# Attention followed by two feed-forward blocks: decode of the first weights begun at unit 11, a step at every second unit until unit 38

## The chip, the cores and the metric

The kernel runs on one core of a Trainium2 chip. The metric is the time of one execution on the device, in microseconds (us). The engines are named as the profile names them: PE is TensorE's matmul and PEld its weight load, DVE is VectorE, ACT is ScalarE, POOL is GpSimd, and SP is SyncE, which here only issues DMAs.

## The reference

Twelve heads of causal attention over two sequences of 448 positions are followed by two blocks of layer norm and a feed-forward network, the second with a Fourier transform in front of it. The two weights of the second block come as float64.

```python
attn = softmax(mask(q @ k.T / sqrt(64))) @ v      # 2 x 12 heads, 448 positions, 64 wide
x = heads side by side                            # 2 x 448 x 768
xn = layer_norm(x) * g
x = x + relu(xn @ w1) @ w2                        # 768 -> 3072 -> 768
u = x + real(fft(fft(x, axis=1), axis=2))
un = layer_norm(u)
out = u + relu(un @ w3) @ w4
```

## The kernel before

All products are kept near float32 accuracy by splitting each operand into a high and a low part and multiplying three times (lines 93 to 95, `mm3`).

**Weights.** They arrive as float64 bits in 96 tiles of 128 x 768 and are turned into two float32r halves by `w_tile`, a generator of four steps: step 1 is an ACT scaling copy (L164) and a DVE shift (L165), step 2 a DVE instruction (L167), step 3 another (L171), step 4 an ACT copy (L89, the high half) and a DVE subtraction (L90, the low half). `w_load` issues the DMA of one raw tile (`wraw`, L147) on the SP queue, 768 KB each. `w_step` runs one step and then loads ahead; `w_tick(n, upto)` runs up to n steps while fewer than `upto` tiles are begun. Raw tiles and the query, key and value tiles of a head pair (`qkv`, `load_pair`) share six slots of one pool, `praw`; the working bits (`wbits`) have two, the finished halves (`wsp`) six.

**Attention.** There are 12 pairs of heads and four units in each pair, so 48 units; the loop runs over `i`, one unit each. A unit's scores (`sps`, L279) get their row minimum on DVE (L296, with `maskw`, in the fourth unit with `maskf`), the exponentials on ACT (`pexp`, L308), transposes on PE (`tps`, L345), a copy on ACT (`pT`, L350), and the product with the values on PE (`avps`, L364). Once a pair, DVE forms the reciprocal row sums (L316, L317), POOL spreads them on a diagonal (`diag`, L322), PE turns these into rows (`invps`, L334), ACT copies them (`inv`, L339), and DVE scales the values (L389) and adds to the sum for the layer norm (`lnacc`, L414). Splitting the queries is work for POOL (L238, L239, L242), splitting the keys for ACT and DVE (`ks`, L250, L251). There is one bank for `avps`: the next pair's values wait for L389.

In the last third of the loop the layer norm of the first sequence runs beside it (`lnm` L428, `xc` L436, `xn` L456 and L466). Here too, in the kernel before, the loads of the first weights begin (from unit 32) and their decode (a step per unit from unit 38). After the loop the first matmuls of the feed-forward block (`hps`, L93 to L95) use the first five tiles, and in their midst stands the layer norm's sum for the second sequence (`lnm`), which needs the last L414.

**Order.** A scheduler places the instructions of each engine while the kernel is built: it follows the program's order as a priority but moves an instruction whose inputs it expects earlier into a place that it expects empty. So a decode step of unit 38 can stand beside unit 31. On the chip each engine runs its list in order and waits at its head.

Of the kernel before, what the change touches and what calls it, by code (L numbers as in the profile page):

```python
# [28 lines left out]
UNITS = [((0, 0, 0, 0, 0), (0, 2, 0, 128, 128)), ((1, 0, 0, 0, 0), (1, 2, 0, 128, 128)),  # L29
         ((0, 1, 0, 0, 0), (1, 1, 1, 0, 256)), ((None, 3, 0, 0, 0),)]  # L30
ES = 4
W_LOAD, W_FROM, W_EARLY = 32, 38, 6
SPLIT_AT = {1: (1, 1), 2: (2, 5)}
AHEAD, L_T, L_C, L_V = (3, 1, 2, 3)
Q_AT, K_AT = (0, 1)
# [17 lines left out]
def fused_kernel(ctx: ExitStack, tc: tile.TileContext, aps, out):  # L53
# [86 lines left out]
    n_raw, n_split = [0], [0]  # L140
# [47 lines left out]
    def w_tick(n=3, upto=None):  # L188
        for _ in range(n):
            if w_now or n_split[0] < min(w_low[0] + WSLOTS, upto or len(order)):  # L190
                w_step()
# [26 lines left out]
    def load_pair(b, pr):  # L218
        t = praw.tile([P, 2 * NM * P], F32, tag="r", name="qkv")
        q_raw[b, pr] = t[:, : 2 * S].rearrange("p (a s) -> p a s", a=2)  # L220
        v_raw[b, pr] = t[:, 2 * S : 2 * S + 8 * D].rearrange("p (r k d) -> p r k d", r=2, k=4)
        if (b, pr) == pairs[0]:
            nc.scalar.dma_start(out=q_raw[b, pr][:, 1], in_=aps["qk"][b, pr][:, 1])
            nc.sync.dma_start(out=q_raw[b, pr][:, 0], in_=aps["qk"][b, pr][:, 0])
        else:
            nc.sync.dma_start(out=q_raw[b, pr], in_=aps["qk"][b, pr])
        nc.sync.dma_start(out=v_raw[b, pr], in_=aps["v2"][b, pr])
# [60 lines left out]
    def row_max(i):  # L288

        b, pr, unit = units[i]  # L290
        if i % len(UNITS) == 0:
            stat[b, pr] = psm.tile([P, 3, NT], F32, tag="st", name="stat")
        for col, at, c, _, n in widths(unit):
            o = s_ps[i][at][:, c : c + n]
            mask = maskf if unit[0][0] is None else maskw
            last = nc.vector.tensor_tensor_reduce(  # L296
                out=o, in0=o, in1=mask[:, mask.shape[1] - n :], scale=1.0, scalar=1e38, op0=ALU.add, op1=ALU.min,
                accum_out=stat[b, pr][:, 0, col : col + 1],
            )
        return last  # L300

    def exps(i):
        b, pr, unit = units[i]
        e = exp_tiles[i % ES]
        flat = e.rearrange("p a b -> p (a b)")
        sp, st = s_ps.pop(i), stat[b, pr]
        for col, at, c, to, n in widths(unit):
            nc.scalar.activation(  # L308
                out=flat[:, to : to + n], in_=sp[at][:, c : c + n], func=ACTF.Exp, scale=-1.0, bias=st[:, 0, col : col + 1],
                accum_out=st[:, 1, col : col + 1],  # L310
            )
        p_sb[i] = e
# [28 lines left out]
    def transposes(i):  # L341
        e = p_sb.pop(i)
        tp = bank("tps")
        for a in range(4):
            nc.tensor.transpose(out=tp[:, a * P : (a + 1) * P], in_=e[:, a], identity=ident)  # L345
        t_ps[i] = tp

    def transposed(i):
        t = t_tile([P, 4, P], "pT", F32)
        nc.scalar.activation(  # L350
            out=t.rearrange("p a q -> p (a q)"), in_=t_ps.pop(i), func=ACTF.Copy
        )
        pT[i] = t
# [336 lines left out]
    i = 0  # L690
    while i < n + L_V or max(later, default=0) >= i:
        pi, at = divmod(i, per)
        if 0 <= i - L_T < n:
            transposes(i - L_T)
        while scored <= min(i + AHEAD, n - 1) and units[scored][:2] in kparts:
            scores(scored)
            scored += 1
        if i < n:
            red = row_max(i)
        if 0 <= i - L_C < n:  # L700
            transposed(i - L_C)
        for f in later.pop(i, []):
            f()
        if i == 0:
            exps(0)
        for f, p in splits.pop(i, []):
            for _ in f(*pairs[p]) or ():
                pass
        if at == 2 and pi + 3 < len(pairs):
            load_pair(*pairs[pi + 3])  # L710
        if i >= W_LOAD and n_raw[0] < n_split[0] + 2:
            w_load()
        if i >= W_FROM:
            w_tick(1, W_EARLY)
        with tc.issue_after(red.ins):
            bg_step()
        if 0 < i < n:
            exps(i)
        if 0 <= i - L_V < n:
            values(i - L_V)  # L720
            b, pr, _ = units[i - L_V]
            if (i - L_V) % per == per - 1:
                scaled(b, pr)
                ln_sum(b, pr, xa)
                if pr >= HJ:
                    later.setdefault(i + 1, []).append(lambda b=b, pr=pr: moved(b, pr))
                if (b, pr) == (0, PAIRS[-1]):
                    later.setdefault(i + 1, []).append(lambda: ln_first())
        if i < n and i % per == per - 1:
            b, pr, _ = units[i]  # L730
            later.setdefault(i + 1, []).append(lambda b=b, pr=pr: (sum_recip(b, pr), spread(b, pr)))
            later.setdefault(i + 3, []).append(lambda b=b, pr=pr: spread_rows(b, pr))
        i += 1
# [138 lines left out]
```

## Time and profile before

| What | us |
|---|---|
| median of three runs (860.02 to 862.39) | 860.39 |
| the profiled execution | 860.33 |
| its span, first to last instruction | 858.6 |
| start of the fourth unit's row minimum, pair 3 (of 0 to 11) | 24.62 |
| last L317 of the attention | 106.07 |
| first matmul of the feed-forward block | 110.02 |
| DVE busy over the span | 602.6 (70%) |
| PE busy over the span | 842.1 (98%) |

PE's busy share is modelled from pipelined matmuls and is no sign of work at its peak. To read the start of the kernel, cut it at the fourth unit's row minimum of each pair (L296 with `maskf`, which is the same instruction in each pair): these lie at 24.62, 32.53, 40.55, 48.58, 56.20, 65.20, 74.41, 82.51, 93.65 and 102.17 us, and a pair's stretch is what lies between two of them. I count them as stretch 3 (24.62 to 32.53) to stretch 11 (93.65 to 102.17). What comes after 110 us is one block of matmuls after another, to the end of the span.

### The profile page before, as it was taken

The numbers are of one execution on the slowest core, as the hardware profiler recorded it, in microseconds if no ns is written. First come the engines' busy times: TensorE is split into PE (matmuls) and PEld (weight loads), VectorE is DVE, ScalarE is ACT, GpSimd is POOL, SyncE is SP. The second block draws the span as 40 slices with busy tenths as digits, with TensorE's granted clock in tenths as the row PEclk, the third lists the DMA queues.
The fourth block names the chain that finished last, engine by engine and source line by source line (L and its number), as shares of the span: only waits on it lengthen the run. The fifth ranks groups of instructions, "written<-read, shape, count | busy, mean of one in ns | idle before, by whom it ended". The sixth has DMA issues, their size and how long they took to land.

```text
span 858.6 us, 11890 instructions
## 1 busy us (share of the span) xinstructions
PE 842.1 (98%) x4688; PEld 754.7 (88%) x4688; DVE 602.6 (70%) x995; ACT 329.3 (38%) x615; POOL 70.5 (8%) x102
## 2 busy tenths in 40 slices
PE   6999899999999999999999999999999999999997
PEld 5766689999999999999998889899999999999997
DVE  5779999796666666656699789697666566666433
ACT  6889874323332233223333245322332233223200
POOL 5665300100000000000100000100000000000000
PEclk9999899999999999999999999999999999999999
DMA  5433444424333333332625202324333333320011
GB/s 202 136 105 130 164 180 148 146 74 148 111 111 111 110 111 107 110 101 95 216 73 197 74 1 87 134 69 151 100 104 108 104 104 110 111 74 0 1 65 65
DMA packets 21399, 93.25 MB, mean 109 GB/s; under 512 B 2750, under 2 KB 4550, under 8 KB 21344
## 3 DMA queue, kind: packets, MB, share of 16 engines
q1 hardware_dynamic: 19152, 86.68, 29.5%
q0 software_dynamic: 2048, 5.59, 2.1%
q8 instruction: 37, 0.61, 0.3%
q10 hardware_dynamic: 144, 0.23, 0.1%
q14 instruction: 18, 0.15, 0.1%
HBM read 88.36 MB, written 2.75 MB: 106 GB/s over the span
## 4 chain that ended last, share of the span: by engine, by line
PE 90%; DVE 4%; ACT 4%; issue 1%; DMA 0%; ACTq 0%; DVEq 0%
PE yps L93 14%; PE yps L95 14%; PE yps L94 14%; PE hps L95 14%; PE hps L93 14%; PE hps L94 14%; ACT pexp L308 2%; PE sps L279 1%; PE avps L364 1%; PE tps L345 1%; DVE sps L296 1%; ACT pT L350 1%; PE mixps L93 1%; PE mixps L94 1%; PE mixps L95 1%
## 5 line engine op out<-in xcount | busy, mean ns | idle before, releaser
L93 PE MATMUL yps<-h,wsp 128*128 128x448 f32 x576 | 211.2, 367 | 0.0
L93 PE MATMUL hps<-xn,wsp 128*128 128x448 f32 x576 | 211.0, 366 | 0.0
L95 PE MATMUL hps<-xn,wsp 128*128 128x448 f32 x576 | 210.9, 366 | 0.0
L94 PE MATMUL yps<-h,wsp 128*128 128x448 f32 x576 | 210.7, 366 | 0.0
L94 PE MATMUL hps<-xn,wsp 128*128 128x448 f32 x576 | 210.5, 366 | 0.0
L95 PE MATMUL yps<-h,wsp 128*128 128x448 f32 x576 | 210.4, 365 | 0.0
L89 ACT ACTIVATE wsp<-wbits 128x768 fp32r<-128x768 f32 x96 | 80.8, 842 | 174.4 <-PE yps L95 159.2
L164 ACT ACTIVATE wbits<-wraw 128x768 f32<-128x768 f32 x96 | 86.3, 899 | 96.5 <-DVE wsp L90 96.5
L93 PEld LDWEIGHTS hps<-xn,wsp 128*128 128x128 f32 x576 | 108.2, 188 | 9.3 <-issue 0.4
L94 PEld LDWEIGHTS yps<-h,wsp 128*128 128x128 f32 x576 | 108.2, 188 | 9.1 <-issue 0.6
L95 PEld LDWEIGHTS hps<-xn,wsp 128*128 128x128 f32 x576 | 108.2, 188 | 9.1 <-issue 0.2
L94 PEld LDWEIGHTS hps<-xn,wsp 128*128 128x128 f32 x576 | 108.2, 188 | 9.0 <-issue 0.2
L93 PEld LDWEIGHTS yps<-h,wsp 128*128 128x128 f32 x576 | 108.2, 188 | 8.9 <-issue 0.4
L95 PEld LDWEIGHTS yps<-h,wsp 128*128 128x128 f32 x576 | 108.2, 188 | 8.8 <-issue 0.2
L507 ACT ACTIVATE h<-hps 128x448 fp32r<-128x448 f32 x96 | 52.0, 543 | 149.7 <-PE hps L95 149.6
L508 DVE SCALAR_TENSOR_TENSOR h<-hps,h 128x448 fp32r<-128x448 f32 x96 | 59.3, 620 | 69.6 <-ACT h L507 69.5
L90 DVE TENSOR_TENSOR wsp<-wbits,wsp 128x768 fp32r<-128x768 f32 x96 | 94.2, 981 | 19.0 <-ACT wsp L89 14.1
L529 DVE TENSOR_TENSOR x<-x,yps 128x448 f32<-128x448 f32 x96 | 58.8, 616 | 68.3 <-PE yps L95 68.3
L165 DVE TENSOR_SCALAR wbits<-wbits 128x768 uint32<-128x768 uint32 x96 | 53.5, 557 | 63.4 <-ACT wbits L164 62.7
L167 DVE SCALAR_TENSOR_TENSOR wbits<-wraw,wbits 128x768 uint32<-128x768 uint32 x96 | 91.7, 955 | 2.3
L171 DVE SCALAR_TENSOR_TENSOR wbits<-wraw,wbits 128x768 uint32<-128x768 uint32 x96 | 92.0, 959 | 0.5
L308 ACT ACTIVATE pexp<-sps,stat 128x128 f32<-128x128 f32 (+3 forms) x84 | 42.0, 516 | 11.6 <-DVE stat L296 11.0
(116 smaller groups left out, 665.1 us busy)
## 6 DMA issues: line engine op xcount, KB each, us to landing
wraw<-in_w SPq DMA_DIRECT2D x96, 768.0 KB, 4.2
qkv<-in_qk SPq DMA_DIRECT2D x11, 448.0 KB, 5.4
qkv<-in_v SPq DMA_DIRECT2D x12, 256.0 KB, 5.8
out_t<-x SPq DMA_DIRECT2D x12, 224.0 KB, 1.9
x<-xr POOLq DMA_DIRECT2D x6, 222.2 KB, 3.4
cd<-in_cd POOLq DMA_DIRECT2D x3, 386.0 KB, 4.1
sd<-in_sd POOLq DMA_DIRECT2D x3, 386.0 KB, 5.9
cs<-in_cs POOLq DMA_DIRECT2D x2, 448.0 KB, 5.8
```

The costliest lines, as they stand in the source:

```text
L89: nc.scalar.activation(out=hi, in_=src, func=ACTF.Copy)
L90: nc.vector.tensor_tensor(out=lo, in0=src, in1=f32(hi), op=ALU.subtract)
L93: nc.tensor.matmul(out=dst, lhsT=w_lo, rhs=x_hi, start=first, stop=False)
L94: nc.tensor.matmul(out=dst, lhsT=w_hi, rhs=x_lo, start=False, stop=False)
L95: nc.tensor.matmul(out=dst, lhsT=w_hi, rhs=x_hi, start=False, stop=last)
L164: nc.scalar.activation(out=f, in_=high.bitcast(F32), func=ACTF.Copy, scale=EXPONENTS)
L165: nc.vector.tensor_scalar(out=bits, in0=bits, scalar1=3, scalar2=None, op0=ALU.logical_shift_left)
L167: nc.vector.scalar_tensor_tensor(out=bits, in0=high, scalar=0x80000000, in1=bits, op0=ALU.bitwise_and, op1=ALU.bitwise_or)
L171: nc.vector.scalar_tensor_tensor(out=bits, in0=low, scalar=29, in1=bits, op0=ALU.logical_shift_right, op1=ALU.bitwise_or)
L308: nc.scalar.activation(out=flat[:, to : to + n], in_=sp[at][:, c : c + n], func=ACTF.Exp, scale=-1.0, bias=st[:, 0, col : col + 1], accum_ ...
L508: nc.vector.scalar_tensor_tensor(out=t[:, 1], in0=src, scalar=0.0, in1=f32(t[:, 0]), op0=ALU.max, op1=ALU.subtract)
L529: nc.vector.tensor_tensor(out=xx, in0=xx, in1=y, op=ALU.add)
```

## The change

A constant is added and two conditions are widened:

```diff
-W_LOAD, W_FROM, W_EARLY = 32, 38, 6
+W_LOAD, W_TWO, W_FROM, W_EARLY = 10, 32, 38, 6
...
-        if i >= W_LOAD and n_raw[0] < n_split[0] + 2:
+        if i >= W_LOAD and n_raw[0] < n_split[0] + (2 if i >= W_TWO else 1):
             w_load()
-        if i >= W_FROM:
+        if i >= W_FROM or i > W_LOAD and i % 2:
             w_tick(1, W_EARLY)
```

The first raw tile is now asked for at unit 10, and at units 11, 13, ... 37 one step of the decode is run; from unit 38 there is one per unit as before. Still at most six tiles are begun in the loop. Fourteen steps are added ahead of unit 38, which is three and a half tiles; with these, all six are decoded inside the loop. Nothing is computed that was not computed before.

The scheduler's lists change with it. The first place is on DVE in stretch 3, behind the fourth unit's row minimum (`stat` rows are the second half of a row minimum). Before:

```order
L251 SCALAR_TENSOR_TENSOR ks<-qkv,ks 128x448
L316 TENSOR_SCALAR stat<-stat 128x7
L317 RECIPROCAL stat<-stat 128x7
L296 ISA sps,stat<-sps,maskw 128x128
L296 ISA stat 128x1
```

and now:

```order
L251 SCALAR_TENSOR_TENSOR ks<-qkv,ks 128x448
L165 TENSOR_SCALAR wbits<-wbits 128x768
L167 SCALAR_TENSOR_TENSOR wbits<-wraw,wbits 128x768
L296 ISA sps,stat<-sps,maskw 128x128
L296 ISA stat 128x1
L316 TENSOR_SCALAR stat<-stat 128x7
```

Two decode instructions of the first tile stand ahead of the row minima of the next pair now, and a third, L171, behind the stretch's L389.

The second place is the end of the attention on DVE, from the last fourth unit's row minimum on. Before:

```order
L296 ISA sps,stat<-sps,maskf 128x448
L296 ISA stat 128x1
L90 TENSOR_TENSOR wsp<-wbits,wsp 128x768
L165 TENSOR_SCALAR wbits<-wbits 128x768
L167 SCALAR_TENSOR_TENSOR wbits<-wraw,wbits 128x768
L316 TENSOR_SCALAR stat<-stat 128x7
L171 SCALAR_TENSOR_TENSOR wbits<-wraw,wbits 128x768
L317 RECIPROCAL stat<-stat 128x7
L165 TENSOR_SCALAR wbits<-wbits 128x768
L389 TENSOR_TENSOR x<-avps,inv 128x448
L90 TENSOR_TENSOR wsp<-wbits,wsp 128x768
L414 TENSOR_TENSOR lnacc<-lnacc,x 128x448
```

and now:

```order
L296 ISA sps,stat<-sps,maskf 128x448
L296 ISA stat 128x1
L171 SCALAR_TENSOR_TENSOR wbits<-wraw,wbits 128x768
L165 TENSOR_SCALAR wbits<-wbits 128x768
L167 SCALAR_TENSOR_TENSOR wbits<-wraw,wbits 128x768
L389 TENSOR_TENSOR x<-avps,inv 128x448
L316 TENSOR_SCALAR stat<-stat 128x7
L171 SCALAR_TENSOR_TENSOR wbits<-wraw,wbits 128x768
L414 TENSOR_TENSOR lnacc<-lnacc,x 128x448
L317 RECIPROCAL stat<-stat 128x7
L389 TENSOR_TENSOR x<-avps,inv 128x448
L414 TENSOR_TENSOR lnacc<-lnacc,x 128x448
```

L389 and the L414 of the pair before the last stand ahead of the last L317 now, not behind it, and no decode stands any more between the last L317 and the last L414.

The third place is the SP queue from the load of pair 5 on. `DMAHW6` and `DMAHW7` are the lanes of the DMAs; in the list of now the first raw tile takes lane 6 and the second lane 7. Before:

```order
L226 DMA qkv<-in_qk 128x896 [waits DMAHW4_49]
L227 DMA qkv<-in_v 128x512 [waits DMAHW5_49]
L226 DMA qkv<-in_qk 128x896 [waits DMAHW6_49,DVE_49,PE_49]
L227 DMA qkv<-in_v 128x512 [waits DMAHW7_49]
L226 DMA qkv<-in_qk 128x896 [waits DMAHW0_49,DVE_49,PE_49]
```

and now:

```order
L226 DMA qkv<-in_qk 128x896 [waits DMAHW4_49]
L227 DMA qkv<-in_v 128x512 [waits DMAHW5_49]
L147 DMA wraw<-in_w_0 128x1536 [waits DMAHW6_49,DVE_49,PE_49]
L147 DMA wraw<-in_w_0 128x1536 [waits DMAHW7_49,DVE_49,PE_49]
L226 DMA qkv<-in_qk 128x896 [waits DMAHW0_49,DMAHW6_49,DVE_49,Activation_49]
```

The load of pair 6 (the third row of before, the last of now) had a slot that an earlier pair gave up; it takes that of the first raw tile now, and so waits until ACT and DVE have decoded that tile.

## Rows read from the trace of the kernel before

**Rows 1.** Stretch, length, busy us (xcount) of PE, PEld, DVE, ACT, POOL, clock, DMA.

```profile
24.62:65.20 40.58, 39.73 (x441) 28.92 (x437) 30.31 (x99) 34.54 (x109) 26.66 (x35) 1.00 0.37 115
65.20:102.17 36.97, 33.48 (x342) 24.59 (x340) 36.40 (x95) 32.15 (x87) 17.60 (x18) 0.91 0.47 163
102.17:106.07 3.90, 3.90 (x51) 2.81 (x48) 3.87 (x9) 3.90 (x12) 0.00 (x0) 1.00 0.12 48
```

**Rows 2.** The same view of one stretch of the feed-forward block.

```profile
170.00:180.00 10.00, 10.00 (x51) 9.27 (x50) 10.00 (x16) 1.75 (x2) 0.00 (x0) 1.00 0.01 2
```

**Rows 3.** Chain that ended last, in time order: start us, us, what.

```profile
84.96 1.49 DVE ks L251
...
89.55 1.83 DVE wsp L90
91.38 0.54 DVE xr L389
```

**Rows 4.** DVE by form, 24.62 to 106.07 us: busy us, mean ns, idle before.

```profile
L251 DVE SCALAR_TENSOR_TENSOR ks<-qkv,ks 128x448 fp32r<-128x448 f32 x8 | 6.8, 846 | 4.3 <-ACT ks L250 4.0 <-POOL zd L242 0.3
...
L466 DVE SCALAR_TENSOR_TENSOR xn<-xc,g_sb,xn 128x448 fp32r<-128x448 f32 x6 | 5.6, 930 | 0.3 <-ACT xn L456 0.3
...
L90 DVE TENSOR_TENSOR wsp<-wbits,wsp 128x768 fp32r<-128x768 f32 x3 | 4.3, 1419 | 0.0
L171 DVE SCALAR_TENSOR_TENSOR wbits<-wraw,wbits 128x768 uint32<-128x768 uint32 x4 | 3.9, 978 | 0.1
L414 DVE TENSOR_TENSOR lnacc<-lnacc,x 128x448 f32<-128x448 f32 x4 | 3.8, 958 | 0.1
L167 DVE SCALAR_TENSOR_TENSOR wbits<-wraw,wbits 128x768 uint32<-128x768 uint32 x4 | 3.8, 955 | 0.1
...
L165 DVE TENSOR_SCALAR wbits<-wbits 128x768 uint32<-128x768 uint32 x4 | 2.2, 552 | 0.0
```

**Rows 5.** The same view, 130 to 850 us.

```profile
L90 DVE TENSOR_TENSOR wsp<-wbits,wsp 128x768 fp32r<-128x768 f32 x90 | 86.1, 957 | 19.0 <-ACT wsp L89 14.1
...
L414 DVE TENSOR_TENSOR lnacc<-lnacc,x 128x448 f32<-128x448 f32 x8 | 5.0, 622 | 0.1
```

**Rows 6.** Timeline, DVE at 27 us: start us, us, what, [idle before <-releaser].

```profile
27.01 0.82 DVE L251 SCALAR_TENSOR_TENSOR ks<-qkv,ks 128x448 fp32r<-128x448 f32 x1 [1.67 <-ACT ks L250]
```

**Rows 7.** Timeline of the attention's end, DVE, then POOL, then PE.

```profile
106.07 0.20 DVE L317 RECIPROCAL stat<-stat 128x7 f32<-128x7 f32 x1
...
106.61 0.62 DVE L389 TENSOR_TENSOR x<-avps,inv 128x448 f32<-128x448 f32 x1
107.14 1.91 DVE L90 TENSOR_TENSOR wsp<-wbits,wsp 128x768 fp32r<-128x768 f32 x1
...
106.44 1.80 POOL L322 TENSOR_TENSOR diag<-ident,stat 128x896 f32<-128x896 f32 x1 [6.43 <-DVE stat L317]
...
108.64 0.98 PE L334 MATMUL invps<-diag,ones 128*64 128x384 f32 x8
109.40 0.69 PE L364 MATMUL avps<-pT,qkv 128*64 128x64 f32 x16
110.02 0.47 PE L93 MATMUL hps<-xn,wsp 128*128 128x448 f32 x1
```

**Rows 8.** Waits of PE, 110 to 130 us: total us, times, longest.

```profile
PE lnm L428 <- DVE lnacc L414: 0.8, 1, 0.8
```

**Rows 9.** Timelines: pair 6's load and first use; page: KB, us to landing.

```profile
22.06 0.33 SPq L226 DMA_DIRECT2D qkv<-in_qk  x1
...
42.34 0.55 POOL L238 CAST qs<-qkv 128x448 fp32r<-128x448 f32 x1
...
qkv<-in_qk SPq DMA_DIRECT2D x11, 448.0 KB, 5.4
```

**Rows 10.** The view of rows 1, around PE's longest wait.

```profile
86.88:89.61 2.73, 0.09 (x3) 0.01 (x1) 2.73 (x13) 2.17 (x4) 1.59 (x2) 0.92 0.35 92
89.61:96.48 6.87, 6.75 (x39) 5.18 (x39) 6.80 (x13) 5.63 (x18) 2.05 (x3) 0.53 0.61 228
```

## The prediction

> **What bounds the kernel now.** I read the engines by stretch first. In the feed-forward block PE starts 51 matmuls in every 10 us and is never without work [rows 2]; nothing that starts earlier or decodes more ahead makes that shorter. So the change can only move the point where this block begins, 110.02 us [rows 7], and one short wait behind it [rows 8]. The attention before it has two halves. From 24.62 to 65.20 us DVE is busy 30.31 of 40.58 us, so 10.27 are free; from 65.20 to 102.17 it is busy 36.40 of 36.97, and to 106.07 for 3.87 of 3.90 [rows 1]. In the second half DVE sets the pace. The chain of waits says the same: it runs through DVE's list, `ks`, a decode L90, L389 [rows 3], and the next pair's values on PE wait for L389. At the end of the attention it leaves DVE by the last L317, which POOL, PE and the first matmuls follow [rows 7].
>
> So the question is not how long the decode takes but how much DVE work stands ahead of the last L317, and how much of it fits into time that was empty.
>
> **What is moved.** In the list of before, four each of L165, L167 and L171 and three L90 stand ahead of the last L317 (the counts in rows 4). In the list of now it is eight each of the three and six L90: all six tiles, and the bits of two more that the scheduler has pulled up. By stretch, the fifteen more are exactly those in stretches 3 to 7, which had none (four L165, four L167, four L171, three L90); stretches 8 to 11 have eleven now as before, and between the last fourth unit and the last L317 there are four now as before. So the second half and the end are not relieved of decode; the tiles in them are only later ones.
>
> **The cost in DVE time.** Four L165 at 0.552, four L167 at 0.955, four L171 at 0.978 and three L90 at 0.957, as they are where nothing disturbs them [rows 4, 5], are 2.2 + 3.8 + 3.9 + 2.9 = 12.8 us. L389 and L414 of the pair before the last stand ahead of the last L317 now too; L389 takes 0.53 from its start to the next [rows 7], and L414 has the same size: 1.1. Sum: 13.9 us more DVE work ahead of that instruction. Nothing of DVE's leaves the list there.
>
> **What was empty.** From 24.62 to 106.07 us DVE was idle 81.45 - 30.31 - 36.40 - 3.87 = 10.87 us [rows 1]. If every bit of it were filled, the last L317 would come 13.9 - 10.9 = 3.0 us later than before.
>
> It will not all be filled. I walked the new lists of DVE and ACT through stretches 3 to 7 with the durations of before. The wait of 1.67 us for ACT's key copy in stretch 3 [rows 6] has the same instructions in front of it on both engines, so it stays. Then L165 waits about 0.5 for its ACT copy, which now stands ahead of the long exponential; in stretches 4, 5 and 6 L316 waits 0.6 to 0.8 for that exponential, in 5 L90 waits 0.8 for ACT's half, in 6 L165 waits 0.5, in 7 the layer norm waits 0.6 for its mean. That is 6.2 us in all. Some of it disappears where a slower instruction ahead only eats the wait; I take 2 off and keep 4.2. Bounds: 1.7 (only the wait that can't go) and 6.2.
>
> **Collisions with POOL.** DVE's instructions on two operands from memory take longer when POOL works: `ks` 846 ns, L414 958, L466 930, L90 1419 in the attention [rows 4], against 622 for a 128x448 form and 957 for L90 where POOL rests [rows 5]. That is 8 x 0.22 + 4 x 0.34 + 6 x 0.31 + 3 x 0.46 = 6.4 us that are in DVE's busy time before. One L90 shows how it comes about: at 107.14 it runs beside POOL's `diag` and takes 1.91 [rows 7]. Eleven of the fifteen new instructions are on two such operands, and POOL is busy in the half that they go to 26.66 of 40.58 us, 66%, in 35 pieces of 0.76 us [rows 1]; if each that meets one waits out half a piece, that is 11 x 0.66 x 0.38 = 2.8 us. The Trainium skill (SBUF — State Buffer, Who interferes with whom) says that a DVE instruction with two SBUF inputs contends with a GpSimd one that reads SBUF, and that whichever was issued first has the shared ports for its whole length. The L90 at 107.14 agrees with that, and the rule speaks against this change, by about those 3 us on top of the forecast. At the other end the old instructions could happen to meet POOL nowhere, and the whole 6.4 go. I take no change: L90 at 957 in the sum and the old collisions as they were. Bounds: -6.4 and +2.8.
>
> **From the last L317 to the block.** Before, from L317 at 106.07 to the first `hps` at 110.02 there are 3.95 us: POOL's `diag` from 106.44 to 108.24, then PE, which had other values in hand until 108.64 [rows 7]. Now those values are done earlier; `diag` ends 2.17 after L317, `invps` takes 0.76 more to the next start, and the half of the last values that is left behind it some 0.3 of their 0.62: 3.2, a gain of 0.75. Behind the start, PE waited 0.8 for the last L414 [rows 8]; now no decode stands between, L414 is ready within the nine matmuls ahead of `lnm`, and the wait goes. With the gap around it, 0.9.
>
> **Where it costs nothing.** The load of pair 6 was issued at 22.06 and first used at 42.34 [rows 9]. Now it waits for the first tile's L171, near 33 us; with 5.4 us to landing [rows 9] it is there some 4 us ahead of POOL. SP has nothing else to do, but the loads of pairs 7 to 9 queue behind; their uses are later still. Each following raw tile has the slot of the one before and is asked for when that is decoded; its ACT copy then waits up to 1 us in stretches 7 and 8, inside the waits above. If that cover fails, ACT holds the exponentials for as long: 1 us. ACT was busy 34.54 of 40.58 in the first half [rows 1] and gets eight more instructions there, so it has no room either; this is why I don't take the lower bound of the waits.
>
> **The sum.** 13.9 - 10.9 + 4.2 - 0.75 - 0.9 = +5.55 us on the profiled execution of 860.33, so 865.9. The median of before, 860.39, lies 0.06 off. With all bounds on one side it would be 860.33 - 3.35 = 857.0 and 860.33 + 10.35 = 870.7.
>
> **Rivals.**
>
> *The empty time takes it (same).* If DVE hardly waits in stretches 3 to 7 but for the 1.7 us, and collisions fall by 2: 13.9 - 10.9 + 1.7 - 2 - 1.65 = +1.05, so 861.4 (1.65 are the 0.75 and 0.9 from above). For it: DVE's waits there are for ACT, and a decode in such a place is free. Against it: ACT is nearly full itself.
>
> *The jam of the second half goes (faster).* PE's longest wait, 2.73 us from 86.88, has a `ks` of 1.49 and a decode instruction in front of it on DVE, and behind it an L90 of 1.83 [rows 3, 10]; then PE runs 6.87 us at a clock of 0.53. If the rearranged list meets POOL almost nowhere, that is -5.9 of collisions, and waits of 1.7: 13.9 - 10.9 + 1.7 - 5.9 - 1.65 = -2.85, so 857.5. It decides from 5.65 us of collisions less, of 6.4 that there are. Against it: that half has as many decode instructions as before.
>
> *The clock falls at the start of the block (slower still).* With the values done early, PE has nothing for about 2.5 us while POOL makes the last `diag`. The wait at 86.88 was as long, and 6.87 us at 0.53 followed [rows 10], which is the lower of the two levels, 1.2 of 2.4 GHz. In the attention that hid behind DVE; at the start of the block it would cost 6.87 x 0.47 = 3.2 us on top of the forecast: 869.1.
>
> **Chances.** Forecast (865.9, from 863.0 to 868) 0.53, same 0.24, faster 0.12, clock 0.11. A difference of 0.3%, 2.6 us, is about what a measurement of this kernel can tell from no change, so the border lies at 857.8 and 863.0: faster 0.12, same 0.25, slower 0.63. The range leaves out most of the faster rival and the far end of the clock: 858.8 to 869.5.
>
> **What would show it.** In the profile after: the distance between fourth-unit row minima in stretches 3 to 7 grows from 40.58 us in all to 44 or more, with DVE over 90% busy there; stretches 8 to 11 take about as long as before or a little less; the last L317 comes near 113 us and the first `hps` near 116; PE's wait for the last L414 is gone; the feed-forward block after it takes the same time. I am wrong if the first `hps` comes at 112 or earlier, with DVE's idle time in stretches 3 to 7 under 2 us or L90 and `ks` near 0.95 and 0.62; and the size is wrong if PE's clock after `hps` falls.

## The result

The changed kernel is slower: median 871.1 us of four runs (869.44 to 873.35) against 860.4 of four of the kernel before (860.02 to 862.39) beside them, ratio 1.0114 with a 95% interval of 1.0093 to 1.0134. The direction was the predicted one, the time lies above the range.

The profile after is of the run of 873.35 us, with a span of 871.6. The three stretches of rows 1, the columns as there (stretch, length, then busy us and count of PE, PEld, DVE, ACT, POOL, clock, DMA share, GB/s):

```profile
27.45:76.42 48.97, 42.76 (x446) 30.94 (x447) 42.88 (x113) 40.52 (x116) 29.89 (x34) 0.97 0.46 148
76.42:115.14 38.72, 33.66 (x351) 24.10 (x350) 37.97 (x97) 32.88 (x89) 17.62 (x18) 0.96 0.46 158
115.14:120.05 4.91, 4.61 (x62) 3.56 (x62) 4.88 (x11) 3.81 (x11) 0.00 (x0) 1.00 0.43 149
```

Stretches 3 to 7 grew by 8.39 us, 8 to 11 by 1.75, the piece to the last L317 by 1.01: 11.15 us in all. DVE is busy 85.73 us (70.58 before) and idle 6.87 (10.87).

The end of the attention, after (timeline: start us, us, what):

```profile
120.05 0.20 DVE L317 RECIPROCAL stat<-stat 128x7 f32<-128x7 f32 x1
120.42 1.69 POOL L322 TENSOR_TENSOR diag<-ident,stat 128x896 f32<-128x896 f32 x1 [9.63 <-DVE stat L317]
122.16 0.99 PE L334 MATMUL invps<-diag,ones 128*64 128x384 f32 x8 [1.68 <-POOL diag L322]
...
123.31 0.47 PE L93 MATMUL hps<-xn,wsp 128*128 128x448 f32 x1
```

From L317 to the first `hps` it takes 3.26 us where [rows 7] has 3.95. The wait of `lnm` [rows 8] no longer shows among PE's waits, and from `hps` to the end of the span there are 748.29 us (748.58 before).

Another 2.83 us stand ahead of stretch 3, which begins at 27.45 instead of 24.62, though the lists of both kernels are the same up to there. From 16 to 20 us (columns as above), with one group of ten equal matmuls of the scores under each row (timeline: start us, us, what), before:

```profile
16.00:20.00 4.00, 3.84 (x41) 2.81 (x42) 3.69 (x10) 4.00 (x14) 3.85 (x4) 1.00 0.02 4
...
12.65 1.13 PE L279 MATMUL sps<-ks,qs 64*128 64x128 f32 x10
```

and after:

```profile
16.00:20.00 4.00, 4.00 (x28) 3.10 (x29) 2.44 (x10) 2.87 (x8) 3.23 (x3) 1.00 0.00 0
...
13.61 1.97 PE L279 MATMUL sps<-ks,qs 64*128 64x128 f32 x10
```

PE, as busy as before, gets through 28 matmuls instead of 41, and the ten take 1.97 us instead of 1.13; the granted clock is 1.00 in both rows, and what slows PE there is not shown. It is not the change: in the profiles of all kernels below the third row minimum with `maskf` comes either at 24.6 or at 27 to 28.5, with early decode (e_hold2 24.55, the changed kernel 27.45) and without (before 24.62, e_late 28.45). The times of the kernel before fall into two groups as well (nine of twenty at 860.2 to 861.1, eleven at 862.1 to 865.5). So I measure every kernel from the start of stretch 3. There the change costs 844.15 - 833.98 = 10.17 us to the end of the span: 11.15, less 0.69 behind the last L317, less 0.29 behind `hps`.

### The profile page after: what moved, and what is told of

The parts are those of the page before. It is cut to its first block, busy times and chain, and to the rows that moved or that the text cites. A ratio compares the mean times of both kernels' runs of the same rounds, so it can differ in the third digit from the quotient of the medians.

```text
span 871.6 us, 11881 instructions
## 1 busy us (share of the span) xinstructions
PE 847.8 (97%) x4688; PEld 757.4 (87%) x4688; DVE 604.3 (69%) x995; ACT 330.9 (38%) x615; POOL 74.2 (9%) x102
## 4 chain that ended last, share of the span: by engine, by line
PE 89%; DVE 5%; ACT 2%; issue 2%; DMA 1%; POOL 0%; ACTq 0%; POOLq 0%; SPq 0%; DVEq 0%
PE hps L93 13%; PE hps L95 13%; PE hps L94 13%; PE yps L93 13%; PE yps L95 13%; PE yps L94 13%; DVE sps L296 2%; ACT pexp L308 1%; PE sps L279 1%; PE tps L345 1%; PE avps L364 1%; DMA wraw<-in_w 1%; PE mixps L93 1%; PE mixps L94 1%; PE mixps L95 1%
## 5 line engine op out<-in xcount | busy, mean ns | idle before, releaser
L164 ACT ACTIVATE wbits<-wraw 128x768 f32<-128x768 f32 x96 | 86.3, 900 | 96.4 <-DVE wsp L90 93.6
L90 DVE TENSOR_TENSOR wsp<-wbits,wsp 128x768 fp32r<-128x768 f32 x96 | 92.2, 961 | 19.1 <-ACT wsp L89 14.2
L165 DVE TENSOR_SCALAR wbits<-wbits 128x768 uint32<-128x768 uint32 x96 | 57.4, 599 | 65.2 <-ACT wbits L164 64.5
L171 DVE SCALAR_TENSOR_TENSOR wbits<-wraw,wbits 128x768 uint32<-128x768 uint32 x96 | 93.0, 969 | 0.4
```

The source lines that it names most:

```text
L90: nc.vector.tensor_tensor(out=lo, in0=src, in1=f32(hi), op=ALU.subtract)
L164: nc.scalar.activation(out=f, in_=high.bitcast(F32), func=ACTF.Copy, scale=EXPONENTS)
L165: nc.vector.tensor_scalar(out=bits, in0=bits, scalar1=3, scalar2=None, op0=ALU.logical_shift_left)
L171: nc.vector.scalar_tensor_tensor(out=bits, in0=low, scalar=29, in1=bits, op0=ALU.logical_shift_right, op1=ALU.bitwise_or)
```

## The experiments

All from the profiles, in us. "Ahead" is the number of decode instructions on DVE ahead of the last L317, with those in stretches 3 to 7 in brackets; "to L317" and "to the end" begin with stretch 3. The ratio is of the timed runs and has their starts in it; in the other columns the start still shows by some 0.4 us (with nothing early in either, stretches 3 to 7 take 40.58 in the kernel before and 40.22 in e_late, which started late).

| Kernel | ahead | stretches 3–7 | DVE idle there | 8–11 | to L317 | to the end | ratio, 95% interval |
|---|---|---|---|---|---|---|---|
| before | 15 (0) | 40.58 | 10.27 | 36.97 | 81.45 | 833.98 | |
| after | 30 (15) | 48.97 | 6.09 | 38.72 | 92.60 | 844.15 | 1.0114 (1.0093–1.0134) |
| e_loads | 19 (4) | 42.97 | 9.76 | 36.92 | 83.80 | 836.14 | 1.0031 (1.0014–1.0047) |
| e_early1 | 23 (8) | 44.70 | 7.33 | 36.92 | 85.52 | 838.75 | 1.0056 (1.0032–1.0079) |
| e_early2 | 27 (12) | 47.98 | 7.04 | 36.93 | 88.82 | 841.62 | 1.0118 (1.0092–1.0144) |
| e_late | 21 (0) | 40.22 | 9.92 | 41.21 | 86.87 | 838.45 | 1.0086 (1.0062–1.0111) |
| e_behind | 26 (10) | 43.90 | 3.22 | 40.09 | 87.96 | 841.02 | 1.0077 (1.0055–1.0098) |
| e_act | 6 (4) | 43.78 | 8.98 | 36.37 | 82.37 | 834.26 | 1.0000 (0.9983–1.0017) |
| e_hold2 | 8 (8) | 44.72 | 7.32 | 32.33 | 79.26 | 834.35 | 0.9992 (0.9976–1.0007) |
| e_hold3 | 12 (12) | 47.79 | 7.10 | 32.32 | 82.32 | 836.02 | 1.0036 (1.0018–1.0054) |
| e_b_diag | 17 (0) | 39.37 | 10.14 | 35.41 | 80.40 | 830.69 | one run |
| e_a_diag | 29 (15) | 47.44 | 7.63 | 32.98 | 86.06 | 836.20 | one run |
| e_dve | 30 (16) | 50.19 | 7.33 | 40.04 | 92.93 | 844.08 | one run |
| e_bh2x | 8 (8) | 43.36 | 4.55 | 32.31 | 77.89 | 835.37 | 1.0011 (0.9997–1.0025) |
| e_bh3x | 12 (10) | 44.38 | 3.19 | 35.44 | 82.04 | 834.42 | 0.9998 (0.9985–1.0011) |
| e_two | 28 (12) | 50.17 | 9.35 | 39.63 | 95.15 | 846.31 | 1.0111 (1.0088–1.0134) |

### How much, and where: four kernels

**e_loads**, the early transfers without the early steps:

```diff
-        if i >= W_FROM or i > W_LOAD and i % 2:
+        if i >= W_FROM:
```

> The changed kernel with its early loads (raw tiles from unit 10 on) but steps from unit 38 on only, as before. On VectorE 19 instead of 15 decode instructions then stand ahead of the last softmax reciprocal (30 in the changed kernel), 4 of them in stretches 3 and 4. Theory (VectorE's own time sets the end of attention; idle time takes a part of what is added): 4 instructions are 3.5 us, of which the idle time there takes 1.5 to 3, and 1.6 us come back behind the last reciprocal; about 860.5, between 859 and 862. Rival A (the early raw-tile transfers and their queueing are what costs): most of the changed kernel's +10 us stays, 867 or more. Rival B (the 3 us slower start of the changed kernel's profile belongs to the change): the matmuls of the first 18 us run at half rate here too.

The end comes 836.14 - 833.98 = 2.16 us later, and the last L317 2.35: the loss stands ahead of it. The scheduler pulled four decode instructions up into stretches 3 and 4 here, so the transfers aren't alone; what is left for them is read from four kernels below. Rivals A and B fall: the end is far from 867, and the start of this kernel is the quick one.

**e_early1** and **e_early2**, the changed kernel with fewer tiles decoded early:

```diff
-W_LOAD, W_TWO, W_FROM, W_EARLY = 10, 32, 38, 6
+W_LOAD, W_TWO, W_FROM, W_EARLY = 10, 32, 38, 1
```

(and 2 at the end for the second).

> The changed kernel, but the early steps may finish 1 tile instead of 6 ahead of the main loop's own needs: 23 decode instructions on VectorE ahead of the last reciprocal, 8 of them in stretches 3 to 5. Theory: 8 more instructions are 7 us, of which idle time takes about 3, and 1.6 us come back behind the last reciprocal; about +2.5 us, 863 (861 to 865). Rival (any decode among the early pairs costs at once, by the order of ScalarE's and VectorE's waits, not by its amount): near the changed kernel's time, 868 or more.

> As the run before, but 2 tiles: 27 decode instructions on VectorE ahead of the last reciprocal, 12 of them in stretches 3 to 7. Theory: 12 more instructions are 10.4 us, of which idle time takes about 3.5, and 1.6 us come back behind the last reciprocal; about +5 us, 865.5 (863 to 868), between the run with 1 tile and the changed kernel. Rival (not by amount): as the changed kernel.

The last L317 moved by 4.07 and 7.37 us, the end by 4.77 and 7.64. So it goes by the amount, as the theory said, and idle time took what I had put in (2.9 and 3.2 us for 3 and 3.5). What is missing in both are the 1.6 us that I gave back behind the last reciprocal. In stretches 3 to 7 the four kernels with 4, 8, 12 and 15 early instructions (e_loads, these two, the changed kernel) grew by 2.39, 4.12, 7.40 and 8.39 us: 0.60, 0.52, 0.62 and 0.56 for each. A straight line through them has 0.58 us an instruction and nothing at none, so nothing is left for the transfers.

**e_late**, the kernel before with two steps instead of one at each unit from 38:

```diff
-            w_tick(1, W_EARLY)
+            w_tick(2, W_EARLY)
```

> The kernel before, with two steps instead of one at each unit from 38 on, and nothing early: 21 decode instructions ahead of the last reciprocal, and the 6 extra ones stand in stretches 10, 11 and behind, none in stretches 3 to 7. There VectorE has almost no idle time. Theory (VectorE's time, wherever it is added): 6 instructions are 5.2 us, nearly all of it on the path, less 1.6 us behind the last reciprocal; about +3.5 us, 864 (862 to 866). Rival (only the early place hurts, through the pipeline of the pairs 3 to 7): same as before, 860.5.

Its stretches 8 to 11 (columns as above):

```profile
68.67:109.88 41.21, 35.90 (x381) 25.84 (x378) 41.00 (x103) 35.48 (x92) 17.88 (x18) 0.96 0.48 164
```

DVE is busy 41.00 of 41.21 us, and six instructions more moved the last L317 by 5.42: 0.90 each, their whole length. The theory holds; the end moved 4.47, a us more than expected. The medians of all four kernels (863.91, 865.33, 871.32 and 869.52) lie above their expected ranges; where the profile started late (e_early2 by 2.6 us, e_late by 3.8) the start is a part of that. So a decode instruction costs all of its time in the second half and 0.5 to 0.6 us in the first, where I had counted on less.

### Place or amount

**e_behind**, each step held behind the row minima of its unit in the scheduler's order:

```diff
-        if i >= W_FROM or i > W_LOAD and i % 2:
-            w_tick(1, W_EARLY)
+        with tc.issue_after(red.ins):
+            if i >= W_FROM or i > W_LOAD and i % 2:
+                w_tick(1, W_EARLY)
```

> The changed kernel with each step of the decode held behind the row minima of its unit. 26 instead of 30 decode instructions then stand ahead of the last reciprocal, 10 instead of 15 in stretches 3 to 7, and none of the first instructions of a tile (L165) stands between a reciprocal and the row minima behind it. Theory (the place counts: an L165 right behind the reciprocal waits out GpSimd's read of the diagonal tile, 1.8 us instead of 0.55, and holds the next row minima and by them ScalarE's exponentials): every L165 of stretches 3 to 7 at 0.55 to 0.8 us, stretches 3 to 7 grow by 4 us or less against the kernel before (8.4 in the changed kernel), last reciprocal 87 us or less behind the start of stretch 3 (92.6 in the changed kernel, 81.45 before). Rival (the amount alone counts): 11 of 15 added instructions, so 11/15 of the 11.15 us, 89.6 us behind the start of stretch 3.

The waits in stretches 3 to 7 (ACT's longest, then DVE's: us in all, times, longest), first of the kernel before, then of the changed kernel; then the row of these stretches and their waits in this one:

```profile
ACT pexp L308 <- DVE stat L296: 5.0, 5, 1.7
...
DVE ks L251 <- ACT ks L250: 4.0, 3, 1.7
DVE stat L316 <- ACT pexp L308: 2.1, 5, 0.8
```

```profile
ACT pexp L308 <- DVE stat L296: 6.9, 8, 2.5
...
DVE stat L316 <- ACT pexp L308: 2.5, 3, 1.3
DVE ks L251 <- ACT ks L250: 1.3, 1, 1.3
DVE wbits L165 <- ACT wbits L164: 0.9, 2, 0.5
```

```profile
27.38:71.28 43.90, 40.38 (x443) 29.17 (x443) 40.68 (x108) 37.82 (x113) 28.87 (x34) 1.00 0.45 147
```

```profile
ACT pexp L308 <- DVE stat L296: 6.0, 6, 2.1
...
DVE ks L251 <- ACT ks L250: 1.3, 1, 1.3
DVE xc L436 <- ACT mean L430: 0.9, 1, 0.9
DVE wbits L165 <- ACT wbits L164: 0.5, 1, 0.5
```

They grew by 3.32 us, as the theory wanted, with ten instructions: 0.33 each. DVE is busy 10.37 us more than before and gave up 7.05 of its 10.27 idle us; in the changed kernel it was 12.57 more and 4.18 given up. The wait of L316 for the exponentials is gone. That speaks for the place; a pair with the same instructions in both (e_hold2 and e_bh2x, below) shows it. My reason for it, though, was not met: two L165 took 1.65 and 1.19 us here too. And stretches 8 to 11, with thirteen decode instructions instead of eleven, grew by 3.12, so the last L317 came at 87.96, between theory and rival: 6.51 us for eleven more instructions, 0.59 each, no less than in e_loads, e_early1 and e_early2 (0.51 to 0.61).

**e_act** and **e_dve** take away one engine's part of the early decode. In e_act:

```diff
+        if at >= 8:
             nc.vector.tensor_scalar(...)            # L165
             nc.vector.scalar_tensor_tensor(...)     # L167
             nc.vector.scalar_tensor_tensor(...)     # L171
```

> The changed kernel without VectorE's instructions L165, L167 and L171 for the first 8 weight tiles: their exponents aren't put together, so the weights are wrong; transfers, ScalarE's two passes (L164, L89) and VectorE's subtraction (L90) stay where they were. Theory (VectorE is what costs): the last reciprocal comes 81 us or less behind the start of stretch 3, since stretches 8 to 11 lose also what stood there before; 76 to 81 us, and stretches 3 to 7 grow by 2 us or less. Rival (ScalarE's passes among the exponentials cost, or the transfers): stretches 3 to 7 stay at 46 us or more, the last reciprocal 88 us or more behind the start of stretch 3.

In e_dve:

```diff
-        nc.scalar.activation(out=f, in_=high.bitcast(F32), func=ACTF.Copy, scale=EXPONENTS)
+        if at >= 8:
+            nc.scalar.activation(out=f, in_=high.bitcast(F32), func=ACTF.Copy, scale=EXPONENTS)
...
-        split(t[:, 0], t[:, 1], f)
+        if at >= 8:
+            split(t[:, 0], t[:, 1], f)
+        else:
+            nc.vector.tensor_tensor(out=t[:, 1], in0=f, in1=f, op=ALU.subtract)
...
```

> The changed kernel without ScalarE's two passes (L164, L89) for the first 8 weight tiles; VectorE's four instructions of each stay (L165 reads the raw tile, L90 subtracts bits from themselves, so the weights are wrong), 16 of them in stretches 3 to 7. It is the counterpart of the run that took away VectorE's L165, L167 and L171 and kept ScalarE's passes, which left stretches 3 to 7 at 43.8 us. Theory A (VectorE's amount and place count): stretches 3 to 7 at 47.5 us or more (49.0 in the changed kernel, 40.6 before). Theory B (the chain from row minima to exponentials to reciprocal runs over ScalarE, whose two passes of 0.9 us stand in it, and that counts about as much): 43 to 46 us. Theory C (ScalarE's passes are the main cost): 43 us or less.

Stretches 3 to 7 (columns as above), first of e_act, then of e_dve, and one of DVE's waits in e_dve there:

```profile
26.94:70.72 43.78, 40.45 (x443) 29.17 (x443) 34.80 (x101) 40.49 (x116) 27.76 (x35) 1.00 0.55 181
```

```profile
27.12:77.31 50.19, 43.16 (x453) 31.12 (x453) 42.86 (x115) 35.14 (x110) 28.68 (x35) 0.97 0.48 159
```

```profile
DVE wbits L167 <- DMA wraw<-in_w: 2.1, 2, 1.8
```

e_act missed its expectation: with only 4.49 us more DVE work than before, and 8.98 left idle, stretches 3 to 7 still grew by 3.20, and the last L317 came at 82.37 and not at 81 or less. ACT's passes, 5.95 us more, are not free; the rival's 46 and 88 us are as wrong. e_dve, with ACT back at 35.14 us, is no shorter than the changed kernel, as theory A said, but that is no clean proof: 2.1 us are waits for raw tiles, which in the changed kernel show on ACT and not on DVE, and it is a single run. So DVE's part weighs more: of 8.08 us taken from DVE, 5.19 came off these stretches and 2.89 came back as waiting; of 5.38 taken from ACT, none came off.

e_act also says something of stretches 8 to 11. It has nine decode instructions fewer there and DVE 5.81 us less to do, and they are only 0.60 shorter: DVE waits in them 4.9 us for exponentials. What is added there costs its whole length (e_late), but of what is taken away only a tenth is won back here, and half in e_hold2 (below).

### Is it POOL's diagonal?

In stretch 6 of the changed kernel there is a telling place (timeline, lines left out between):

```profile
57.50 0.98 ACT L164 ACTIVATE wbits<-wraw 128x768 f32<-128x768 f32 x1
...
57.91 0.20 DVE L317 RECIPROCAL stat<-stat 128x7 f32<-128x7 f32 x1
...
58.27 1.69 POOL L322 TENSOR_TENSOR diag<-ident,stat 128x896 f32<-128x896 f32 x1 [3.29 <-DVE stat L317]
...
58.51 1.86 DVE L165 TENSOR_SCALAR wbits<-wbits 128x768 uint32<-128x768 uint32 x1 [0.39 <-ACT wbits L164]
...
60.29 0.29 DVE L296 CUSTOM_DVE_ANT_0 sps<-sps,maskw 128x128 f32<-128x128 f32 x1
...
61.49 0.37 ACT L308 ACTIVATE pexp<-sps,stat 128x128 f32<-128x128 f32 x1 [2.53 <-DVE stat L296]
```

L317 releases POOL's diagonal; L165, freed by ACT a moment later, runs beside it for 1.86 us instead of 0.55 [rows 4], the next unit's row minima stand behind, and ACT waits 2.53 us for them. Another L165, at 41.32, took 1.81 the same way. I took this for the missing 4 us and tried it in two ways.

**e_b_diag** and **e_a_diag**: the kernel before and the changed one with one seventh of the diagonal.

```diff
-            out=d, in0=ident.unsqueeze(1).to_broadcast([P, NT, P]),
-            in1=stat.pop((b, pr))[:, 2].unsqueeze(2).to_broadcast([P, NT, P]), op=ALU.mult,
+            out=d[:, 0], in0=ident, in1=stat.pop((b, pr))[:, 2, :1].to_broadcast([P, P]), op=ALU.mult,
```

> The kernel before, with GpSimd's diagonal (L322, 1.7 us) cut to one block of seven, which the products behind it read for all; so the factors of 1/sum are wrong. It is the partner of the next run. Theory and rival: GpSimd's instruction takes 0.2 to 0.5 us instead of 1.7; since none of VectorE's decode instructions stood beside it in stretches 3 to 7 of the kernel before, those stretches stay at 40.6 us, at most 2 us less.

> The changed kernel with the same cut. VectorE's order in stretches 3 to 7 is that of the changed kernel. Theory (an L165 that is released beside the diagonal waits it out, and holds the row minima behind it): with the diagonal short the two L165 of 1.8 us come to 0.9 or less, and stretches 3 to 7 are 6 us or less longer than in its partner (8.4 us between the changed kernel and the kernel before). Rival (amount of work and waits for ScalarE, not the diagonal): 8 us or more longer than in the partner.

Stretches 3 to 7, first of e_b_diag, then of e_a_diag:

```profile
24.61:63.98 39.37, 39.37 (x441) 28.84 (x437) 29.23 (x99) 34.64 (x109) 18.73 (x34) 1.00 0.37 118
```

```profile
27.30:74.74 47.44, 42.77 (x449) 30.87 (x449) 39.81 (x113) 40.37 (x117) 21.23 (x34) 0.96 0.49 159
```

The partner is 1.21 us shorter than the kernel before, as expected. The L165 came down to 0.57 and 0.78 us, and DVE's extra work in these stretches from 12.57 to 10.58. Yet they are 8.07 us longer than in the partner, against 8.39: the rival's number. What DVE saved came back as idle time (7.63, not 6.09). Stretch by stretch it is less clear: where the two L165 stand, in stretches 4 and 6, the distance to the partner fell by 0.61 and 1.26 us, and in 3, 5 and 7 it grew by 0.31, 0.28 and 0.96; in stretch 7 the granted clock was 0.86 here, 0.96 in the changed kernel and 1.00 in the partner. Up to the last L317 the difference is 5.66 instead of 11.15, but there the orders differ too: twelve instructions more than the partner, not fifteen, and in stretches 8 to 11 nine against twelve. Three instructions are 2.7 us at e_late's 0.90; how much of the rest is the diagonal's is open.

**e_two**: only the first instruction of tiles 1 to 3 is moved behind the row minima that follow it.

```diff
+        with tc.issue_after(reds[-3].ins) if 0 < at < 4 else nullcontext():
             nc.vector.tensor_scalar(out=bits, in0=bits, scalar1=3, scalar2=None, op0=ALU.logical_shift_left)
...
             red = row_max(i)
+            reds.append(red)
```

> The changed kernel with the first decode instruction (L165) of the early tiles 1 to 3 held behind the row minima that stand behind it in the changed kernel; TensorE's order is unchanged, VectorE keeps all its decode instructions. Theory (an L165 right behind a reciprocal waits out the diagonal, holds the row minima and starves ScalarE): L165 in stretches 4 and 6 at 1 us or less, stretches 3 to 7 at 46 us or less (49.0 in the changed kernel, 40.6 before), last reciprocal 89.5 us or less behind the start of stretch 3 (92.6). Rival (amount): 48 us or more, 92 us or more.

In its listing the instruction is line 166:

```profile
42.05 1.15 DVE L166 TENSOR_SCALAR wbits<-wbits 128x768 uint32<-128x768 uint32 x1
...
62.09 0.82 DVE L166 TENSOR_SCALAR wbits<-wbits 128x768 uint32<-128x768 uint32 x1
```

They are shorter (the first not down to the 1 us expected), and nothing is won: stretches 3 to 7 take 50.17 us, with twelve decode instructions there, since the scheduler put three others behind them. The profiled clock was lower here (0.90 in these stretches, 0.97 in the changed kernel), but the timed runs (869.38 to 875.64) are no better than those of the changed kernel either. The clock is an unlikely cause: e_early2 and e_hold3 have the same twelve instructions in stretches 3 to 7, clocks of 1.00 and 0.96, and take 47.98 and 47.79 us. As the cause of the bulk of the first half's loss the theory of the diagonal falls; up to the 1.9 us of stretches 4 and 6 are not excluded.

### What the late decode is worth

Four kernels decode some tiles early and hold all the rest on DVE until the attention is over. **e_hold2** and **e_hold3** hold it behind the last L317:

```diff
-W_LOAD, W_TWO, W_FROM, W_EARLY = 10, 32, 38, 6
+W_LOAD, W_TWO, W_FROM, W_EARLY = 10, 32, 38, 2
...
+        with tc.issue_after(last_recip[0].ins) if held[0] else nullcontext():
             if w_now and next(w_now[0], "end") == "end":
                 w_now.pop()
...
     raw_ahead[0] = 2
+    held[0] = True
```

(with 3 for the second).

> The changed kernel with 2 tiles decoded early (8 instructions in stretches 3 to 5) and all other decode held on VectorE behind the last reciprocal, so none in stretches 6 to 11. Theory (a decode instruction costs its duration where VectorE has no idle time, stretches 8 to 11 and the piece behind, and about half of it in stretches 3 to 5): +4.1 us as in the run with 1 tile, less most of the 12.6 us of the 15 instructions that stood in stretches 8 to 11 and behind: last reciprocal 75 us (73 to 78) behind the start of stretch 3, 6.5 us ahead of the kernel before. Against it: with 2 tiles instead of 3 to 4 decoded at the last reciprocal the first products behind it may wait for weights, and give back up to 5 us. Total 857 (852 to 862).

> As the run before with 3 tiles: 12 instructions in stretches 3 to 7, none in 8 to 11. Theory: +7.4 us in stretches 3 to 7 as in the run with 2 early tiles, less most of 12.6 us: last reciprocal 77.5 us (75 to 80) behind the start of stretch 3; total 857 (853 to 861), less risk of waiting for weights behind the last reciprocal than with 2 tiles. Rival (the early work costs more than the late work it takes away): 861 or more.

The last L317 came at 79.26 and 82.32, later than the 75 and 77.5 expected: without decode stretches 8 to 11 shrank by 4.6 us, though eleven instructions had left them; DVE is idle there for 5.11 now. e_hold3's median, 865.41, lies where its rival has it (861 or more). And e_hold2, 2.19 us ahead at the last L317, gives that back at once (timeline; L391 is L389 of before):

```profile
103.81 0.20 DVE L319 RECIPROCAL stat<-stat 128x7 f32<-128x7 f32 x1
...
103.93 2.47 DVE L165 TENSOR_SCALAR wbits<-wbits 128x768 uint32<-128x768 uint32 x2
...
106.32 0.61 DVE L391 TENSOR_TENSOR x<-avps,inv 128x448 f32<-128x448 f32 x1
```

Two L165 went ahead of the L391 for which PE's next values waited, and the first `hps` comes 5.91 us behind the last reciprocal (3.95 before); in the block PE waits another 1.1 us for a weight tile.

**e_bh2x** and **e_bh3x** cure that: the steps stand behind their unit's row minima as in e_behind, and the hold is the next to last L389.

```diff
+        with tc.issue_after(scales[-2].ins) if held[0] else nullcontext():
             if w_now and next(w_now[0], "end") == "end":
                 w_now.pop()
...
+        scales.append(nc.vector.tensor_tensor(out=xt, in0=av.pop((b, pr))[:, :S], in1=inv.pop((b, pr)), op=ALU.mult))
```

> The changed kernel with 2 tiles decoded early, each step behind its unit's row minima, and all other decode held on VectorE behind the next to last product with 1/sum (L389) instead of the last reciprocal, which the runs with a hold showed to be 2 us too early (two L165 beside the diagonal, 2.47 us, ahead of the L389 for which TensorE waited). 8 decode instructions in stretches 3 to 6, none in 7 to 11. Theory (place and not amount): stretches 3 to 7 at 43 us or less, last reciprocal 78 us or less behind the start of stretch 3 (81.45 before), first product with weights 4 us behind it; total 4 us ahead of the kernel before, 856.5 (854 to 859.5). Rival (what is decoded late is missed later, as with the hold at the reciprocal): 860 to 862.

> As the run with 2 tiles behind the row minima and the hold at the next to last product with 1/sum, but 3 tiles decoded early, so 12 decode instructions in stretches 3 to 8 and none in 9 to 11. Theory (the 2.7 us that TensorE waited for a weight tile in the run with 2 tiles go, and the third tile costs about 2 us among the pairs): last reciprocal 80 us (79 to 81) behind the start of stretch 3, no wait of TensorE for weights; from the start of stretch 3 to the end 833 us (832 to 834.5), as before (834.0) or 1 us less; total 859.5 (858 to 861) where the start is as before. Rival (the wait for weights is DVE's total work, which 4 instructions more ahead don't mend): 835 us or more from the start of stretch 3.

e_bh2x brings the last L317 to 77.89 and `hps` to 82.36 us behind the start of stretch 3, 3.04 earlier than the kernel before, and loses 4.43 in the block. PE's waits from `hps` on, and the three us behind the wait (columns as above):

```profile
PE hps L93 <- DVE wsp L90: 2.7, 1, 2.7
...
124.77:127.80 3.03, 3.03 (x8) 2.76 (x9) 3.03 (x5) 2.47 (x4) 0.00 (x0) 0.50 0.37 87
```

The wait is 2.7 us, and behind it the granted clock was 0.50, the lower of its two levels, for 3 us, which is worth some 1.5 more (an estimate, 3 x 0.5). The median, 863.56, lies above the expected range and the rival's; stretches 3 to 7, 43.36, just missed their 43.

With three tiles that wait is gone; the last L317 is at 82.04, 2 us later than expected, and the end at 834.42, within the expected range and 0.44 behind the kernel before. None of the four beats it. Set side by side, e_hold2 and e_bh2x have the same eight instructions early and differ in stretches 3 to 7 by their place alone: 44.72 us with 7.32 idle, and 43.36 with 4.55. The same list differs far less from profile to profile (e_early1 and e_hold2 44.70 and 44.72, e_early2 and e_hold3 47.98 and 47.79), so the place counts for about 1.4 us, of which up to 0.4 can be the later start of e_bh2x.

## Why the prediction was wrong

**What bounds the kernel: right for what is added.** The second half goes by DVE when work is added to it (e_late), though not when work is taken away (e_act); the block from `hps` on goes by PE (748.29 and 748.58 us), and weights that are decoded sooner than PE needs them buy nothing there. The direction followed from this and was no luck.

**What is moved, and its price: nearly right.** 13.9 us of added DVE work were forecast, and DVE was busy 15.15 us more.

**Collisions: mis-sized.** I took no change and counted only two-operand instructions as exposed. The changed kernel's DVE by form, over stretches 3 to the last L317:

```profile
L165 DVE TENSOR_SCALAR wbits<-wbits 128x768 uint32<-128x768 uint32 x8 | 8.2, 1036 | 0.9 <-ACT wbits L164 0.9
...
L90 DVE TENSOR_TENSOR wsp<-wbits,wsp 128x768 fp32r<-128x768 f32 x6 | 6.1, 1011 | 0.1
```

L165, with one operand, was priced at 0.552 and took 1.036 on average: 3.9 us for eight. L90 fell from 1.419 [rows 4] to 1.011, so the net is 15.15 - 13.9 = +1.25, inside the bounds; that it came out so small is the luck of two errors against each other. The Trainium skill (SBUF — State Buffer, Who interferes with whom) says that `tensor_scalar`, too, can enter two-port modes in which it contends with GpSimd, besides the forms with two inputs; the L165 of 1.81 and 1.86 us beside the diagonal agree.

**The waits that are kept: the step that failed.** The walk through the lists gave 6.2 us; I took 2 off because "a slower instruction ahead only eats the wait", and kept 4.2. It was 6.87, over the upper bound: 6.09 in stretches 3 to 7, which is what the walk had, nearly item by item (L316's waits 2.5 us for 2.1, the key copy's 1.3 for 1.67, L165's 0.9 for 1.0; 0.8 for L90 didn't show, 0.8 for L389 and L296 wasn't forecast), and 0.78 behind them, where the walk didn't go and the sum counted the 0.60 of before as filled. So nothing of the 2 us disappeared. The prediction had a reason in hand, an ACT with no room, and used it against the lower bound only. My reading is that DVE and ACT wait for each other: ACT's waits for row minima grew from 5.0 to 6.9 us, while DVE's for the exponentials stayed (2.1 and 2.5). That behind the row minima less idle time stays fits this (e_bh2x 4.55 us for e_hold2's 7.32); it is not shown by itself. The step makes 2.7 of the 4.6 us by which the sum fell short (5.55 for 10.17); the DVE work makes 1.25, the two gains behind the last L317 0.7.

**Behind the last L317: right, and then a third.** 0.69 for 0.75, and 0.29 for 0.9; the wait of `lnm` went, and the block kept 0.6 of it.

**Where it costs nothing: nearly.** A copy L164 was to wait up to 1 us for its raw tile in stretches 7 and 8; it waited 0.4 us in 7 and 2.4 in 8, with DVE idle for only 0.75 us in stretches 8 to 11.

**The sum.** 860.33 + 15.15 - 10.87 + 6.87 - 0.69 - 0.29 = 870.5, beside a median of 871.1 that mixes two starts. With the walk's own 6.2 and no discount the forecast would have been 867.9. The median lies even above the 870.7 of all bounds on one side; part of that is the late start, but without it, too, the time is above the range.

**The rivals.** *The empty time takes it* had the waits at 1.7 and failed with them. *The jam of the second half goes*: stretches 8 to 11 were 1.75 us longer. *The clock falls at the start of the block*: PE did wait for the diagonal, 1.68 us, but `hps` took 0.47 as before, and the granted clock stayed at 1.00. What that rival feared does happen behind a longer wait (e_bh2x: 2.7 us, then 0.50).

**What would show it.** Stretches 3 to 7 at 44 us or more: 48.97. DVE over 90% busy there: 88%. Stretches 8 to 11 no longer: no, 38.72 for 36.97; with eleven decode instructions as before DVE was busy 1.57 longer. Last L317 near 113: 120.05, or 117.2 without the later start.

**Open.** That the place of a step decides how much idle time it fills is measured (0.33 to 0.38 us for a step instruction behind its unit's row minima, 0.52 to 0.62 where the scheduler pulled it up). Which of the pulled-up places does the harm is not: moving the three L165 did not help, and the shorter diagonal helped in two stretches and not in their sum.

## What to carry to other kernels

Idle time inside a loop over several engines is only in part room: here work put into 10.3 us of it lengthened the loop by 0.58 to 0.82 of what it kept DVE busy, and by 0.32 to 0.35 in the best order that I found. Walk the new order and believe the waits that come out, without a discount; then put the filler behind what the other engines are waiting for. And before starting work earlier, look whether anyone waits for it: here no wait for weights shows on PE in the kernel before.

## Unexpected on the hardware

- A single-operand DVE instruction (L165) took 1.81 and 1.86 us beside POOL's diagonal (1.94 in e_loads), and 0.55 alone: it is drawn out as much as a two-operand one (L90, 1.91 in [rows 7]).
- Without any decode in stretches 8 to 11 (e_hold2) their length fell from 36.97 to 32.33, though DVE was busy 9.18 us less: it was idle for 5.11 us, 3.7 of them in waits for the exponentials.
- The same list starts at two speeds: 41 or 42 matmuls in the four us from 16 on, or 21 to 32, at a granted clock of 1.00 in the rows. Between the profiles this moves everything behind it by 2.3 to 3.9 us.
- After PE had waited 2.7 us in the block (e_bh2x), its granted clock was 0.50 for the next 3 us; after 1.68 us at the start of the block (the changed kernel) it stayed at 1.00.
